# Infini-attention beside an FNet block: new times for the projections' helper work, a new table of a group's operations, another block order at the end

## The chip, the cores and the metric

The kernel runs on one core of a Trainium2 chip. The metric is the device time of one execution in microseconds (us). A core has a matrix engine (TensorE; PE in the profile, PEld for its weight loads), a vector engine (DVE), a scalar engine (ACT), a general engine (POOL) and a queue engine that issues the transfers (SP). Each engine takes its instructions strictly in the order in which they stand in its own queue, and an instruction that waits holds up all that stand behind it.

## What is computed

Two independent blocks over 2048 rows of 576 features, whose results are laid side by side. Cut to what matters:

```python
# A: 32 heads of 18, 4 segments s of 512 rows
q, k, v = x @ wq, x @ wk, x @ wv
for s in range(4):
    logits = q_s @ k_s.T * scale + mask   # mask: -1e9 where the key comes after the query
    a_dot  = softmax(logits) @ v_s
    a_mem  = (phi(q_s) @ M) / (phi(q_s) @ z + 1e-6)
    o_s    = g * a_mem + (1 - g) * a_dot
    M, z   = M + phi(k_s).T @ v_s, z + sum(phi(k_s))
out_A = concat(o_s) @ wo
# B
a, b  = xB @ hid_re.T, xB @ hid_im.T
out_B = seq_re @ a - seq_im @ b
```

The result has to be close to float32. So most operands are cut into a high and a low half, high by a copy to a narrower type on ACT, low by a subtraction on DVE or POOL, and a product is two or three matrix multiplications.

## The kernel before

Three stages follow each other.

**Projections (0 to about 237 us of the span).** For each of the four segments: nine products of queries and keys (`project_qk`, L368 and L148, the copy out of PSUM at L426) and four blocks of values (`project_v`, L483 to L495), with the memory's sums (`accumulate`, L522), the lookup in it (`lookup`, L555 to L576) and a transposed copy of the keys for it (`k_natural`, L464, which reads the key tiles `kf` that L426 writes). Each segment has 13 ticks: nine for the products, four for the value blocks. Beside this main line there is helper work with a written time each, in ticks from the start: load, high and low half of the other block's input (`fourier_load`, `fourier_high` L295 on ACT, `fourier_low` L300 on DVE), high and low half of the keys (L396 ACT, L402 DVE) and of the queries (L393 and L394 ACT, L400 POOL), load and split of the next segment's input (`x_load`, `split_x`: L121 ACT, L122 DVE). The table `TIMES` holds these times. They are sorted into one agenda, and after each tick `timed` issues all that is due, so the table alone decides behind which main instructions a piece of helper work stands on its engine.

**Attention and the Fourier block together (about 237 to 895 us).** Attention works on 32 groups of four heads, the Fourier products are a stream of matrix multiplications (`dense`: first `hidden`, L858 to L868, then `sequence`, L814, evacuated at L879). A group step has 16 slots. `PLACE` gives each operation of a group a place in slots, and 16 more mean one step later. In each slot the operations due are issued, and then as much of `dense` as keeps the two streams even. So the table also decides how many dense multiplications lie between two attention multiplications on PE. `PLAN` holds a few extra pieces by slot: among them the load and split of the second set of hidden weights (`h_load`, `h_split`, L594).

The path of one group, named as in the table:
- `run_1` to `run_4` are what PE does: scores (L1202) into the PSUM banks `s` and `t`, two of each. `run_1` writes f1 and s0, `run_2` f0 and s1, `run_3` s2, f2 and the transposed scores t1 (L1287), `run_4` t0 and t2. A run waits until the readers of its banks are done. `run_2` and `run_4` also hold the sums with the values (L1334, L1335), `run_4` ends with a small transposition of the maxima.
- `f_min`, `s_min` (L1210, DVE) take row minima from PSUM; `f_exp` (L1232, L1236, ACT) follows `f_min` and leaves `pf`.
- `f_hi` (L1244, ACT) and `f_lo` (L1249) cut `pf` into the tile `hl`. `f_turn` (L1253) transposes a half of `hl` by a transfer from SP's queue into `ptt`. There is one `hl` for each half, so the next group's `f_hi_1` waits for that transfer.
- `maxima` (POOL) and `maxima_out` (L1270, ACT) hand the row maxima to the transposed side, whose bank `t` they read.
- `t_exp` (L1294, L1298, ACT), `t_mask` (L1302, POOL), `t_hi` (L1307, ACT) and `t_lo` (L1314) make `phi` and `plo` for the sums with the values.
- `pv_read` (L1341, L1342, DVE) and `pv_out` (POOL, L1351 to L1357) finish a head.
- `stacks`, `values`, `memory` are loads. `c_cut` (L645 ACT, and its low half on POOL, which runs from the line of the delayed calls, L192) prepares the next operand `cs` of the dense stream, about five times in a step.

`LOW` says which of DVE and POOL makes each low half. Before, `f10`, `f11`, `f21`, `t20` and `t21` were POOL's, the rest DVE's.

**Output (about 911 to 971 us).** The product with `wo` by seventh-part sums (L1100). Then the branch: a flag `passed` is loaded, and if it is 0 the Fourier block is computed again in a general way (`fourier_by_words`). With the inputs here the flag is 1 and the block is skipped.

Of the kernel before, what the change touches and what calls it, by code (L numbers as in the profile page):

```python
# [101 lines left out]
def infini_attention_and_fnet(ctx: ExitStack, tc: tile.TileContext, xT, wqk, w8, wv, wo, beta, xbT, cT, hT, out):  # L102
# [582 lines left out]
    def value_load(G):  # L685
        if G < NG:
# [3 lines left out]

    TIMES = {
        "fourier_load": [
            2.22, 2.55, 6.61, 6.23, 11.7, 12.08, 14.63, 15.65, 19.32, 18.99, 22.59, 22.5, 24.9, 26.14, 28.77, 29.86,
            34.38, 33.5, 36.97, 36.61],
        "fourier_high": [
            3.55, 5.07, 8.15, 7.45, 13.2, 13.58, 16.57, 16.92, 21.57, 20.49, 24.09, 24.66, 27.16, 27.59, 30.27, 31.36,
            35.09, 35.6, 38.47, 38.32],
        "fourier_low": [
            4.72, 5.52, 9.13, 8.76, 13.83, 14.45, 18.15, 17.99, 21.9, 21.58, 24.28, 25.96, 27.52, 27.84, 31.66, 32.51,
            36.55, 36.26, 39.65, 38.97],  # L700
        "key_high": [
            6.72, 12.35, 9.68, 12.09, 5.49, 22.11, 19.18, 22.09, 26.12, 21.34, 33.23, 34.06, 38.2, 37.41, 33.04, 45.1,
            45.51, 50.28, 48.1, 44.1],
        "key_low": [
            7.72, 12.69, 10.68, 13.09, 6.98, 22.12, 25.68, 23.09, 26.75, 21.83, 34.6, 38.89, 41.52, 37.46, 34.47,
            46.1, 46.51, 51.28, 51.89, 45.1],
        "query_high": [
            6.49, 7.59, 12.09, 11.79, 19.0, 23.0, 23.22, 25.91, 33.32, 39.28, 33.75, 37.62, 45.14, 46.73, 50.47, 48.38],
        "query_low": [
            8.39, 7.92, 12.86, 11.89, 19.1, 23.33, 23.95, 26.32, 33.42, 39.38, 33.85, 38.03, 45.24, 46.83, 50.57,  # L710
            48.48],
        "x_load": [
            8.47, 8.76, 9.32, 10.61, 11.01, 15.83, 16.51, 19.4, 22.78, 24.1, 26.63, 31.84, 32.51, 33.4, 33.84],
        "x_split": [
            9.78, 10.88, 24.46, 24.08, 30.02, 32.47]}
    AGENDA = []

    def begin_cut(what, n):
# [715 lines left out]
    for i in BOTH:  # L1434
# [7 lines left out]
    WORK["stacks"], WORK["values"], WORK["memory"] = stack_load, value_load, memory_load  # L1442

    PLACE = {
# [8 lines left out]
    LOW = {k: (dve, pool)[n] for k, n in {  # L1453
        "f00": 0, "f01": 0, "f10": 1, "f11": 1, "f20": 0, "f21": 1, "t00": 0, "t01": 0, "t10": 0, "t11": 0, "t20": 1,
        "t21": 1}.items()}

    def attention():
# [45 lines left out]
    output_stage(prepare)  # L1503
    stages.close()
    rv = nc.values_load(passed, min_val=0, max_val=1)
    with tc.If(rv < 1, preferred_fallthrough_block=False):
        fourier_by_words(tc, dma, xbT, cT, hT, out)


# [41 lines left out]
```

## Time and profile before

| | |
|---|---|
| time, median of 3 runs | 972.62 us (972.52 to 977.6) |
| the profiled execution | 972.7 us, of which the span from first to last instruction is 970.9 us |
| PE busy | 925.2 us, 95% of the span |
| DVE, ACT, POOL busy | 738.6, 695.9, 652.5 us |
| mean granted clock of TensorE | 0.987 |

How to read it: a row of a group names the line, the engine, the operation and the tiles, then how often, the busy time in us and the mean length in ns, then the idle time just before and who ended it. A row of the waits says who waited for whom, the sum in us, how often, and the longest. A row of a timeline has the start in us, the length, the instruction, and in brackets how long the engine stood idle before it and who released it. PEclk is the granted clock of TensorE as a share of its full one. PE's own busy time counts overlapping ends of its multiplications, so a PE that is busy all the time still has the pace of its multiplications as its limit.

### The profile page before, as it was taken

To read this page: it belongs to the slowest core of one execution; us is meant where nothing else is said; L and a number is where in the kernel's file an instruction comes from. 1 tells how busy PE (TensorE), PEld (TensorE's weight loads), DVE (VectorE), ACT (ScalarE), POOL (GpSimd) and SP (SyncE) were. 2 spreads that over 40 slices of the span, in tenths; PEclk is the share of its full clock that TensorE was granted. 3 is DMA by queue.
4 is the path that set the end of the run, shared out by engine and by line. 5 is a ranking of instruction groups with operands and counts; after the bars stand their busy time and mean duration, and the time that the engine had idled before them with its cause. 6 is when DMAs were issued, how large, how long until landed. Compare 5 with 4: busy or idle time off the path is not lost.

```text
span 970.9 us, 25747 instructions
## 1 busy us (share of the span) xinstructions
PE 925.2 (95%) x9288; PEld 737.4 (76%) x9288; DVE 738.6 (76%) x1994; ACT 695.9 (72%) x1665; POOL 652.5 (67%) x954
## 2 busy tenths in 40 slices
PE   9999898998899999999899999999999999999996
PEld 8988888987677777777677777777776767777896
DVE  7777876877787777787677877777777788886783
ACT  6777757675576777887678788788778877886341
POOL 1566655676233335886778888878878998878560
PEclk9999998999999999999999999999999999999999
DMA  8565655656857655777797987888889797776552
GB/s 259 174 195 157 223 167 166 220 166 239 232 111 162 136 127 145 166 182 183 181 210 177 208 215 186 180 206 211 183 210 225 191 205 181 192 183 144 165 171 86
DMA packets 283129, 177.69 MB, mean 183 GB/s; under 512 B 204881, under 2 KB 240977, under 8 KB 282961
## 3 DMA queue, kind: packets, MB, share of 16 engines
q1 hardware_dynamic: 282768, 175.82, 70.9%
q8 instruction: 75, 1.23, 0.5%
q14 instruction: 62, 0.50, 0.2%
q10 hardware_dynamic: 224, 0.14, 0.1%
HBM read 90.00 MB, written 44.83 MB: 139 GB/s over the span
## 4 chain that ended last, share of the span: by engine, by line
PE 47%; ACT 17%; POOL 13%; DVE 8%; DMA 8%; issue 6%; SPq 0%; POOLq 0%; DVEq 0%; ACTq 0%
PE d L814 17%; DMA ptt<-hl 4%; PE d L858 3%; PE qk L368 3%; ACT pd L1298 3%; PE d L859 3%; PE d L860 3%; POOL cs L192 3%; PE t L1100 2%; PE pv L1334 2%; PE v L148 2%; ACT hl L1244 2%; ACT phi L1294 2%; ACT cs L645 2%; DVE s L1210 2%
## 5 line engine op out<-in xcount | busy, mean ns | idle before, releaser
L814 PEld LDWEIGHTS <-cs 128*128 128x128 f16 x3072 | 293.6, 98 | 89.4 <-issue 18.0
L814 PE MATMUL d<-wide,cs 128*128 128x288 f16 x2592 | 338.8, 287 | 4.5 <-ACT y L879 4.5
L1210 DVE CUSTOM_DVE_ANT_0 s<-s,causal 128x384 f32<-128x384 f32 (+2 forms) x320 | 147.2, 501 | 87.0 <-PE s L1202 57.4
L1249 POOL TENSOR_TENSOR hl<-pf,hl 128x512 f16<-128x512 f32 (+1 forms) x96 | 101.1, 1061 | 116.0 <-ACT hl L1244 106.1
L192 POOL TENSOR_TENSOR cs<-craw,cs 128x512 f16<-128x512 f32 x128 | 157.5, 1236 | 31.5 <-ACT cs L645 25.5
L1236 ACT ACTIVATE pf<-s,nb 128x384 f32<-128x384 f32 (+3 forms) x256 | 117.4, 525 | 3.2
L1244 ACT ACTIVATE hl<-pf 128x512 f16<-128x512 f32 (+1 forms) x192 | 94.0, 555 | 14.1 <-DMA ptt<-hl 13.9
L1249 DVE TENSOR_TENSOR hl<-pf,hl 128x512 f16<-128x512 f32 (+1 forms) x96 | 80.6, 874 | 30.5 <-ACT hl L1244 29.4
L1210 DVE CUSTOM_DVE_ANT_0 t<-t,causal 128x384 f32<-128x384 f32 (+1 forms) x192 | 98.9, 543 | 2.2
L645 ACT ACTIVATE cs<-craw 128x512 f16<-128x512 f32 x128 | 80.6, 634 | 2.3 <-PE d L814 2.3
L1294 ACT ACTIVATE phi<-t 128x384 f16<-128x384 f32 x128 | 63.7, 498 | 13.0 <-PE t L1287 9.5
L1232 ACT ACTIVATE nb<-nb 128x2 f32<-128x2 f32 (+1 forms) x96 | 19.5, 203 | 66.4 <-DVE nb L1210 66.3
L814 PE MATMUL d<-ab,cs 128*128 128x288 f16 x480 | 66.2, 286 | 0.0
L1314 POOL TENSOR_TENSOR plo<-pd,phi 128x384 f16<-128x384 f32 x64 | 58.3, 926 | 2.4 <-ACT pd L1298 2.4
L1202 PEld LDWEIGHTS <-st 54*128 54x128 f16 x512 | 20.3, 94 | 49.3 <-issue 43.3
L148 PE MATMUL v<-wide,xh 128*128 128x288 f32 x256 | 54.7, 306 | 0.4 <-ACT r L426 0.4
L1314 DVE TENSOR_TENSOR plo<-pd,phi 128x512 f16<-128x512 f32 x64 | 53.7, 870 | 1.5 <-ACT phi L1307 1.4
L868 ACT ACTIVATE wide<-d 128x288 f16<-128x288 f32 x54 | 22.3, 415 | 35.5 <-PE d L865 35.4
L1302 POOL TENSOR_SCALAR_AFFINE_SELECT pd<-pd 128x512 f32<-128x512 f32 x64 | 44.7, 721 | 0.3 <-ACT pd L1298 0.2
L368 PE MATMUL qk<-xh,wide 128*128 128x512 f32 x128 | 44.1, 401 | 0.0
L1314 DVE TENSOR_TENSOR plo<-t,phi 128x384 f16<-128x384 f32 x64 | 33.6, 553 | 12.9 <-ACT t L1298 12.6
L148 PEld LDWEIGHTS v<-wide,xh 128*128 128x128 f32 x256 | 41.9, 193 | 1.0 <-ACT r L426 0.6
(329 smaller groups left out, 2466.2 us busy)
## 6 DMA issues: line engine op xcount, KB each, us to landing
craw<-cT SPq DMA_DIRECT2D x128, 256.0 KB
vd<-vs SPq DMA_DIRECT2D x16, 440.0 KB
vst<-vd SPq DMA_DIRECT2D x32, 220.0 KB
st<-qd SPq DMA_DIRECT2D x64, 108.0 KB
st<-kd SPq DMA_DIRECT2D x64, 108.0 KB
wide<-xbT SPq DMA_DIRECT2D x20, 256.0 KB
xk<-xd SPq DMA_DIRECT2D x20, 256.0 KB
out<-y SPq DMA_DIRECT2D x16, 288.0 KB
```

What stands on the lines that cost most here:

```text
L148: pe.matmul(o, a, b, start=n == 0, stop=n == len(terms) - 1)
L192: fn(*a)
L368: pe.matmul(FIRST[m], *terms[m][n], start=n == 0, stop=n == 13)
L645: act.activation(t[:, 0], raw, AF.Copy)
L814: pe.matmul(o[h], a, b[:, h * 288:h * 288 + 288], start=start, stop=stop)
L1210: dve.tensor_tensor_reduce(x, x, CAUSAL[0][:, L - w:], scale=scale, scalar=-LOWEST, op0=OP.add, op1=OP.min, accum_out=into[:, 4 * half + i ...
L1236: act.activation(f[kind][half][:, to:to + w], o[half][:, c:c + w], AF.Exp, bias=nb[:, 4 * half + i:4 * half + i + 1], scale=-1.0)
L1244: act.activation(hl[half][:, 0, F_COL[kind]:F_COL[kind + 1]], f[kind][half], AF.Copy)
L1249: engine.tensor_tensor(hl[half][:, 1, a:b], f[kind][half], hl[half][:, 0, a:b], OP.subtract)
L1294: act.activation(t[0][:, a:a + 384], x, AF.Exp, bias=LIFT, scale=SCALE)
L1302: pool.affine_select(v, v, pattern=[[0, 4], [1, P]], base=0, channel_multiplier=-1, compare_op=OP.is_ge, fill=0.0)
L1314: engine.tensor_tensor(lo[:, a:b], f, hi[:, a:b], OP.subtract)
```

## The change

Three things change, and no instruction of the computation is added or left out.

1. All the times in `TIMES` are new, most by less than a tick, some by two to five ticks.
2. `PLACE` is new, and in `LOW` the low halves f10, f11 and f21 go from POOL to DVE, t00 and t01 from DVE to POOL.
3. The block of the branch that is never taken here is placed directly behind the main block, where before the empty block was.

```diff
     TIMES = {
...
         "x_split": [
-            9.78, 10.88, 24.46, 24.08, 30.02, 32.47]}
+            9.48, 11.3, 19.05, 24.61, 32.55, 34.01]}
...
     PLACE = {
-        "stacks": -10.31, "run_1": 1.0, "f_min_1": 1.1, "s_min_0": 2.05, "f_exp_1": 3.7, "run_2": 6.0, "f_min_0": 6.1,
...
+        "stacks": -8.87, "run_1": 1.4, "f_min_1": 1.74, "f_exp_1": 2.61, "s_min_0": 4.8, "run_2": 5.08, "f_min_0":
...
     LOW = {k: (dve, pool)[n] for k, n in {
-        "f00": 0, "f01": 0, "f10": 1, "f11": 1, "f20": 0, "f21": 1, "t00": 0, "t01": 0, "t10": 0, "t11": 0, "t20": 1,
+        "f00": 0, "f01": 0, "f10": 0, "f11": 0, "f20": 0, "f21": 0, "t00": 1, "t01": 1, "t10": 0, "t11": 0, "t20": 1,
         "t21": 1}.items()}
...
-    with tc.If(rv < 1, preferred_fallthrough_block=False):
+    with tc.If(rv < 1, preferred_fallthrough_block=True):
         fourier_by_words(tc, dma, xbT, cT, hT, out)
```

In the new file every line behind the first table has a number higher by one, so L1249 of before is L1250 now.

What it does to the order shows best at three places. The rows are instructions of one engine in the order of its queue, with the line, the operation, and out<-in by tile names.

**The third segment's last products, on ACT.** `kf` is the copy of a product out of PSUM, the last of the four being the one that `k_natural` needs first. Before:

```order
L295 ACTIVATE p<-wide 128x512
L426 ACTIVATE kf<-qk 128x512
L121 ACTIVATE xh_136<-raw 128x512
L426 ACTIVATE kf<-qk 128x512
L396 ACTIVATE p<-kf,sc 128x512 x2
L393 ACTIVATE q<-q,sc 128x512
L394 ACTIVATE p<-q 128x512
L393 ACTIVATE q<-q,sc 128x512
L394 ACTIVATE p<-q 128x512
L426 ACTIVATE kf<-qk 128x512
```

The same place now:

```order
L295 ACTIVATE p<-wide 128x512 x2
L426 ACTIVATE kf<-qk 128x512 x2
L396 ACTIVATE p<-kf,sc 128x512
L121 ACTIVATE xh_135<-raw 128x512
L393 ACTIVATE q<-q,sc 128x512
L394 ACTIVATE p<-q 128x512
L426 ACTIVATE kf<-qk 128x512
L396 ACTIVATE p<-kf,sc 128x512
L426 ACTIVATE kf<-qk 128x512
L121 ACTIVATE xh_136<-raw 128x512
```

Between the last but one `kf` and the last there stood two key halves and two query cuts; now one key half stands there, one query cut comes before both, and an input split comes after them.

**The first step of attention, on ACT.** `ab<-raw` at L594 is `h_split`, which waits for a weight load; the `pf` of 128x512 are `f_exp_0`. Before:

```order
L868 ACTIVATE wide<-d 128x288
L594 ACTIVATE ab<-raw 128x576
L868 ACTIVATE wide<-d 128x288
L1232 ACTIVATE nb<-nb 128x2
L1236 ACTIVATE pf_3294<-s,nb 128x512
L1236 ACTIVATE pf_3295<-s,nb 128x512
```

Now:

```order
L869 ACTIVATE wide<-d 128x288 x2
L1233 ACTIVATE nb<-nb 128x2
L1237 ACTIVATE pf_3278<-s,nb 128x512
L1237 ACTIVATE pf_3279<-s,nb 128x512
L594 ACTIVATE ab<-raw 128x576
```

`f_exp_0` has passed the split that waits for a transfer.

**A late group, on DVE, from the last minimum after `run_3` to the end of the step.** `hl` is written by `f_lo`, `plo` by `t_lo`, `pw` and `pa` by `pv_read`. Before:

```order
L1314 TENSOR_TENSOR plo<-t,phi 128x384 x2
L1341 RECIPROCAL pw<-pv 128x8
L1342 TENSOR_REDUCE pa<-pv 128x144
L1249 TENSOR_TENSOR hl<-pf_9498,hl 128x512
L1249 TENSOR_TENSOR hl<-pf_9578,hl 128x256
L1249 TENSOR_TENSOR hl<-pf_9499,hl 128x512
```

Now:

```order
L1250 TENSOR_TENSOR hl<-pf_9374,hl 128x512
L1250 TENSOR_TENSOR hl<-pf_9375,hl 128x512
L1315 TENSOR_TENSOR plo<-t,phi 128x384 x2
L1250 TENSOR_TENSOR hl<-pf_9575,hl 128x256
L1250 TENSOR_TENSOR hl<-pf_9475,hl 128x512
L1250 TENSOR_TENSOR hl<-pf_9476,hl 128x512
L1250 TENSOR_TENSOR hl<-pf_9576,hl 128x256
```

The two low halves f10 and f11 now stand ahead of `t_lo_10` and `t_lo_11`, which free the banks `t` for `run_4`, and f21 has come behind; `pv_read_0` has moved ahead of `run_3`'s minima, and the two `t_lo` of kind 0, which stood on DVE between `run_1` and `run_2`, are POOL's. On PE, the dense multiplications between the runs, on the mean of the groups 8 to 30, go from 35, 28, 27 and 21 (behind `run_1`, `run_2`, `run_3`, `run_4`) to 27, 20, 35 and 28; their sum in each step is the same.

More of the change, by code (lines that the diff above doesn't have):

```diff
@@ L698, in infini_attention_and_fnet @@
+            35.23, 34.44, 38.71, 40.14],
         "fourier_low": [
-            4.72, 5.52, 9.13, 8.76, 13.83, 14.45, 18.15, 17.99, 21.9, 21.58, 24.28, 25.96, 27.52, 27.84, 31.66, 32.51,
-            36.55, 36.26, 39.65, 38.97],
+            4.94, 4.99, 9.42, 7.61, 11.58, 12.85, 18.13, 17.97, 21.45, 21.42, 24.28, 25.96, 27.25, 28.51, 31.81,
+            31.55, 36.51, 34.59, 39.28, 40.59],
         "key_high": [
-            6.72, 12.35, 9.68, 12.09, 5.49, 22.11, 19.18, 22.09, 26.12, 21.34, 33.23, 34.06, 38.2, 37.41, 33.04, 45.1,
@@ L703, in infini_attention_and_fnet @@
-            45.51, 50.28, 48.1, 44.1],
+            7.19, 12.35, 9.7, 13.5, 5.18, 22.47, 19.18, 22.79, 26.59, 21.05, 33.59, 35.2, 38.62, 37.17, 32.23, 45.1,
+            46.49, 50.73, 48.1, 44.1],
         "key_low": [
-            7.72, 12.69, 10.68, 13.09, 6.98, 22.12, 25.68, 23.09, 26.75, 21.83, 34.6, 38.89, 41.52, 37.46, 34.47,
-            46.1, 46.51, 51.28, 51.89, 45.1],
+            7.56, 12.69, 10.84, 15.71, 6.17, 22.51, 26.54, 23.97, 26.87, 21.54, 34.69, 38.89, 41.96, 37.58, 32.39,
+            46.1, 47.97, 51.28, 51.89, 45.1],
@@ L707, in infini_attention_and_fnet @@
         "query_high": [
-            6.49, 7.59, 12.09, 11.79, 19.0, 23.0, 23.22, 25.91, 33.32, 39.28, 33.75, 37.62, 45.14, 46.73, 50.47, 48.38],
+            6.49, 8.34, 12.49, 10.17, 19.12, 25.56, 25.1, 26.13, 32.73, 38.45, 36.68, 37.33, 46.92, 47.19, 49.45,
+            48.01],
         "query_low": [
-            8.39, 7.92, 12.86, 11.89, 19.1, 23.33, 23.95, 26.32, 33.42, 39.38, 33.85, 38.03, 45.24, 46.83, 50.57,
+            6.99, 8.67, 13.26, 10.27, 19.22, 25.89, 25.83, 26.98, 32.95, 38.55, 36.78, 37.74, 50.46, 47.29, 49.55,
@@ L711, in infini_attention_and_fnet @@
             48.48],
         "x_load": [
[L713 removed]
+            8.44, 8.76, 9.32, 10.17, 10.77, 16.17, 16.51, 19.52, 24.06, 24.1, 26.04, 29.19, 31.69, 35.39, 36.94],
         "x_split": [
[L715 removed]
+            9.48, 11.3, 19.05, 24.61, 32.55, 34.01]}
     AGENDA = []
```

7 lines of the change are left out of this document (3 added, 4 removed), and 14 rows, old and new, of the table PLACE.

## The prediction

> **What bounds the kernel now.** I read the page's busy times first, then the stretches by stage, then the waits of PE. The times are those of the profiled execution, 972.7 us around a span of 970.9; the median of the runs, 972.62, is the same to 0.1 us, so a difference worked out here holds for both.
>
> ```profile
> PE 925.2 (95%) x9288; PEld 737.4 (76%) x9288; DVE 738.6 (76%) x1994; ACT 695.9 (72%) x1665; POOL 652.5 (67%) x954
> ```
>
> ```profile
> 0.00:237.00 237.00, 225.64 (x1373) 202.68 (x1374) 181.44 (x360) 166.90 (x365) 140.10 (x218) 0.98 0.61 196
> 237.00:262.00 25.00, 21.43 (x148) 14.74 (x147) 18.88 (x55) 12.71 (x31) 8.34 (x12) 0.86 0.76 236
> 262.00:394.00 132.00, 129.00 (x1456) 97.03 (x1455) 104.84 (x324) 95.54 (x240) 54.51 (x92) 1.00 0.61 137
> 394.00:623.00 229.00, 221.74 (x2660) 164.55 (x2658) 173.47 (x546) 181.07 (x443) 185.01 (x266) 0.99 0.83 193
> 623.00:874.00 251.00, 240.47 (x2884) 178.81 (x2882) 198.85 (x597) 200.27 (x488) 214.94 (x304) 1.00 0.85 197
> ```
>
> PE is the bound in every stage, and the change leaves its multiplications as they are. So all that can be won is PE's idle time: 237 - 225.6 = 11.4 us in the projections, 3.6 in the first step, 3.0 in the seven steps with `hidden`, and 7.3 + 10.5 = 17.8 in the later ones, 36 us in all. Beside it there is time at a lower clock:
>
> ```profile
> 116.00:120.00 4.00, 4.00 (x18) 3.71 (x19) 3.79 (x14) 1.44 (x4) 1.73 (x2) 0.57 0.90 216
> 154.00:161.00 7.00, 6.36 (x28) 6.37 (x29) 3.93 (x8) 4.04 (x11) 4.34 (x7) 0.51 0.90 289
> 253.00:257.00 4.00, 3.69 (x20) 2.21 (x19) 3.43 (x12) 2.48 (x6) 2.84 (x3) 0.57 0.51 137
> 485.00:489.00 4.00, 4.00 (x28) 2.45 (x27) 2.71 (x6) 3.97 (x11) 3.50 (x9) 0.57 1.02 270
> ```
>
> The clock is 0.57 on the mean of 4 us, which is half speed for 3.4 of them: 1.7 us of work lost each time, and 0.49 x 7 = 3.4 us in the long one. Each of these stretches begins beside one of PE's longest waits, as at 485:
>
> ```profile
> 484.02 2.19 PE L814 MATMUL d<-wide,cs 128*128 128x288 f16 x13 [3.82 <-ACT y L879]
> ```
>
> The waits by sum, times and the longest:
>
> ```profile
> PE t L1202 <- ACT mt L1270: 10.6, 18, 1.5
> ACT ab L594 <- DMA raw<-hT: 5.2, 1, 5.2
> PE d L814 <- ACT y L879: 4.5, 3, 3.8
> PE kt L464 <- ACT kf L426: 3.8, 2, 3.2
> PE s L1202 <- ACT pf L1236: 3.1, 4, 2.0
> PE look L561 <- DVE vr L486: 3.0, 3, 2.2
> ```
>
> The waits of 2.2 us (`look`), 3.2 (`kt`), 2.0 (`s`) and 3.8 (`d`) are the four that have a slow stretch behind them; the 18 short ones on `mt` have none. I go through the change by these rows.
>
> **The projections' times.** The `look` wait comes from a heap on DVE at the end of a value block of the second segment:
>
> ```profile
> 111.15 0.68 DVE L122 TENSOR_TENSOR xl<-raw,xh 128x512 fp32r<-128x512 f32 x1
> 111.75 1.66 DVE L300 SCALAR_TENSOR_TENSOR p<-wide,p 128x512 f16<-128x512 f32 x1
> 113.33 1.74 DVE L122 TENSOR_TENSOR xl<-raw,xh 128x512 fp32r<-128x512 f32 x1
> ```
>
> `x_split`'s third time goes from 24.46 to 19.05, so one of the two `xl` leaves this heap for a tick in which DVE had no helper work. That is 0.7 to 1.7 us; the one that goes stands last, so I take 1.7, and half of the slow stretch (0.9), since 0.5 us of wait stays: -2.6.
>
> The `kt` wait is the heap on ACT that the order shows:
>
> ```profile
> 147.93 0.62 ACT L121 ACTIVATE xh<-raw 128x512 fp32r<-128x512 f32 x1
> 150.45 0.72 ACT L396 ACTIVATE p<-kf,sc 128x512 f16<-128x512 f32 x1 [0.81 <-POOL sc L386]
> 154.01 0.58 ACT L426 ACTIVATE kf<-qk 128x512 f32<-128x512 f32 x1
> ```
>
> From the first row to the last are eight operations in 6.1 us, 0.8 of them a wait, so some 0.6 us each. Ahead of the last `kf` one query cut (two operations), a key half and an input split go elsewhere: 2.4 us of the 3.2. With half of the slow stretch, 1.7, that is -4.1. What moved earlier lands in ticks 30 to 32 and DVE's tick 34, which now holds three low halves instead of two; one of about 1 us late at the next `look` would be a wait of its own, and the loads that come up to two ticks earlier meet the weights' loads. I put +2 on both together, between 0 and the 4 us of the waits now removed. The first step:
>
> ```profile
> 250.89 0.68 ACT L594 ACTIVATE ab<-raw 128x576 f16<-128x576 f32 x1 [5.21 <-DMA raw<-hT]
> 252.00 1.26 ACT L1236 ACTIVATE pf<-s,nb 128x512 f32<-128x512 f32 x2
> ```
>
> `f_exp_0` stands behind a split that sat 5.2 us for its load, and `run_3` waits for `f_exp_0` (2.0 and 0.3 us). Now it stands before the split. The split still waits, but behind it are only evacuations `wide<-d`, for which PE has three banks: -2.3, and half of a slow stretch, -0.9.
>
> **The group's table.** On PE the distance from `run_4` to the next `run_1` grows from 21 to 28 dense multiplications. Their pace:
>
> ```profile
> 605.94 3.85 PE L814 MATMUL d<-wide,cs 128*128 128x288 f16 x30
> 609.62 0.90 PE L814 MATMUL d<-ab,cs 128*128 128x288 f16 x6
> ```
>
> 30 in 3.68 us, so 0.123 us each and 0.86 us more for seven. The 18 waits on `mt` (`maxima_out`, which frees bank `t` for s0) are 0.6 us on the mean: nearly all go, -10.6 at most; I take that. These also hold in the `hidden` steps.
>
> The wait of 3.8 us at 480 us begins with a transfer:
>
> ```profile
> ACT hl L1244 <- DMA ptt<-hl: 13.9, 10, 3.5
> ```
>
> `f_hi_1` sat 3.5 us for the other half's transposition, ACT with it, and behind it the cut of the next `cs`. All low halves that `f_turn_0` needs are now done about two slots earlier (2.4 us: 394 to 874 us are 25 steps, 19.2 us for 16 slots) on the queue, `f_hi_1` is asked for one slot earlier. So this wait goes but with one slot of room: -3.8 and half a slow stretch, -0.9.
>
> What is late next is DVE. Between `run_3` and `run_4` it now has two more low halves ahead of `t_lo_10` and `t_lo_11`:
>
> ```profile
> 615.80 0.39 PE L1202 MATMUL s<-st 54*128 54x256 f16 x4
> ```
>
> ```profile
> 617.83 1.02 DVE L1314 TENSOR_TENSOR plo<-t,phi 128x384 f16<-128x384 f32 x2
> ```
>
> ```profile
> L1249 POOL TENSOR_TENSOR hl<-pf,hl 128x512 f16<-128x512 f32 x64 | 73.2, 1156 | 100.4 <-ACT hl L1244 91.9 <-DMA out<-y 3.8 <-DMA craw<-cT 3.8
> L1249 DVE TENSOR_TENSOR hl<-pf,hl 128x512 f16<-128x512 f32 x64 | 64.7, 1012 | 29.5 <-ACT hl L1244 29.4
> ```
>
> The minima are through 617.83 - 615.80 = 2.0 us after `run_3` begins, 2.2 with the next instruction's start; then 2 x 1.01 and 1.02 makes 5.2 us. PE comes to the multiplication that needs the bank after the runs' own 0.5 us, 35 x 0.123 = 4.3, and 0.25 for t0: 5.0. So it waits about 0.2 us in each of 25 steps, +5. Between `run_1` and `run_2` there are 27 multiplications instead of 35, 3.3 us behind 0.9 of `run_1` itself, 4.2:
>
> ```profile
> 623.73 0.39 PE L1202 MATMUL s<-st 54*128 54x384 f16 x4
> ```
>
> ```profile
> 626.45 1.57 ACT L1236 ACTIVATE pf<-s,nb 128x384 f32<-128x384 f32 x4
> ```
>
> `f_exp_1` ended 628.02 - 623.73 = 4.3 us after `run_1` began, so that is even: +0.1 a step, +2.5. `t_lo_00` and `t_lo_01` on POOL:
>
> ```profile
> L1314 POOL TENSOR_TENSOR plo<-pd,phi x64: 903/912/1356, 283.3 to 892.3; 128x384 f16<-128x384 f32 x64
> L1314 DVE TENSOR_TENSOR plo<-pd,phi x64: 650/691/1643, 287.8 to 895.0; 128x512 f16<-128x512 f32 x64
> L1314 DVE TENSOR_TENSOR plo<-t,phi x64: 546/553/559, 276.6 to 886.4; 128x384 f16<-128x384 f32 x64
> ```
>
> Four `t_lo` of 0.9 to 1.2 us and one or two `cs` now stand on POOL before `run_2`'s sums; in an average step they are done, now and then not: +2.5. In sum POOL gives 2 x 1.16 + 0.87 us a step and takes two of about 1.2, DVE gives 2 x 0.87 (mean) and takes 2 x 1.01 + 0.6: DVE goes from 199 of 251 us busy to about 83%, POOL from 86 to 82%. Bounds of these three new waits: 0 if the low halves on DVE run at 0.65 (the shortest row above), and 37 us if each needs 1.64 (the longest): 2.2 + 3.3 + 1.0 = 6.5, 1.5 us late, 25 times. I take +10, near the mean row.
>
> Here the Trainium skill speaks against the change. "SBUF — State Buffer", section "Who interferes with whom", says that a DVE instruction with both inputs in SBUF contends with a GpSimd instruction that reads SBUF, and that the loser is held for the other's whole length. The rows agree: 546 to 559 ns with one input in PSUM, 650 to 1643 with both in SBUF. By that rule with POOL 82% busy in 1.16 us pieces a low half would take some 0.65 + 0.5 = 1.15 us (an estimate), the wait at `run_4` 0.5 us, and the time 967.
>
> **The branch.** One far jump is on SP's path before and after:
>
> ```profile
> L1506 SPq COMPARE_BRANCH x2: 43/50/57, 965.0 to 966.3; - x2
> L1544 SPq EVENT_SEMAPHORE x10: 17/28/28, 969.5 to 970.8; - x10
> ```
>
> The jump takes 969.5 - 966.3 = 3.2 us and came after the wait for the last store (1.3 us from the first branch). Now the jump comes first and the store lands meanwhile: -0.5, between -1.3 and +3.2, the last if the short second jump costs as much.
>
> **The sum.** -2.6 - 4.1 + 2 - 3.2 - 10.6 - 4.7 + 10 - 0.5 = -13.7, from 972.7: 959.
>
> **The rivals.**
> - *DVE becomes the bound between `run_3` and `run_4`* (slower). With a wait of 1.0 us there in 25 steps, instead of 0.2, the sum is -13.7 + 20 = +6: 979. It decides from 0.75 us a step, that is from a low half of 1.3 us. For it speaks the 1.64 us row; against it that the mean with POOL at 85% is 1.01, and that DVE has over a microsecond idle behind `f_lo_21` to catch up. 11 in 100.
> - *The waits only change place* (no change). PE's waits on `mt` come back as waits on `f_min` and `f_exp`, whose distances became shorter, and half of the projections' gain too: -13.7 + 10.6 + 3 = 0: 970 to 973. For it: 0.0 us of room between `run_1` and `run_2`. 17 in 100.
> - *All slow stretches go and DVE keeps up*: the other halves of them, 0.9 + 1.7 + 0.9 + 0.9 = 4.4 us more, and +2 instead of +10: 947. 12 in 100.
> - *The slow stretches don't hang on these waits*: 963, still faster; held in my forecast.
>
> The skill's page "TensorE: Matmul & The Clock Gate", Part 1, says that the clock is halved after an idle window of about 3.4 us. By it the waits of 2.0 and 2.2 us would be too short, their stretches would stay, and the time would be 961; here stretches follow such waits, so I keep the rows.
>
> **How the numbers follow.** My forecast, 950 to 967, has 60 in 100. Less than 0.5% (4.9 us) is what a measurement of this kernel cannot tell from no change. Faster than that: 60 + 12 = 72; within it: 17; slower: 11. The range goes from 948, near the fastest case, to 973, where the case of no change ends; the likeliest alone has 950 to 967.
>
> **What would show it.** Right: no wait of `t` on `mt` over 1 us in total; the wait of `kt` at the third segment under 1 us; no stretch at 0.57 at 253 and at 485; new waits of PE on `plo` from DVE or on bank `t` at `run_4`, some 0.2 us each; low halves f10 and f11 near 1.0 us. Wrong: group steps longer than 19.2 us; DVE over 90% in the last stretch; a new wait over 2 us in the projections, with its own slow stretch.

## The result, and the profile after

The changed kernel takes 959.81 us on the median of four runs (956.91 to 960.03), the kernel before 973.01 beside it (972.52 to 977.6): a ratio of 0.985, with a 95% interval of 0.981 to 0.988. The forecast was 959. The profiled execution is the 956.91 one, with a span of 955.2, so differences between the two traces (15.7 us) are some 2.5 us more than those of the medians. The kernel after has one line more, so its L1203 is L1202 of before, and so on.

The first part of the page, the busy times:

```profile
PE 920.7 (96%) x9288; PEld 731.4 (77%) x9288; DVE 739.8 (77%) x2026; ACT 698.6 (73%) x1665; POOL 629.2 (66%) x922
```

PE is still the bound. The stages, now cut at the starts of the same instructions in both traces (run_1 of step 0, of step 1 and of step 7, the end of the last sums). Columns as in the prediction: the stretch, its length, busy times of PE, PEld, DVE, ACT, POOL, granted clock, DMA share, GB/s. First the kernel before, then the kernel after:

```profile
0.00:237.08 237.08, 225.65 (x1374) 202.68 (x1374) 181.52 (x360) 166.98 (x365) 140.18 (x218) 0.98 0.61 196
237.08:262.14 25.06, 21.56 (x148) 14.74 (x147) 18.94 (x54) 12.63 (x31) 8.40 (x12) 0.86 0.76 237
262.14:394.70 132.56, 129.56 (x1459) 97.42 (x1460) 104.80 (x324) 96.24 (x242) 55.07 (x94) 1.00 0.62 137
394.70:897.63 502.93, 484.38 (x5822) 361.26 (x5822) 386.48 (x1164) 395.93 (x964) 419.47 (x593) 1.00 0.83 193
897.63:970.90 73.27, 64.06 (x490) 61.31 (x488) 46.90 (x94) 24.10 (x65) 29.34 (x41) 0.97 0.44 140
```

```profile
0.00:231.95 231.95, 221.74 (x1373) 198.32 (x1374) 177.41 (x360) 167.18 (x365) 141.17 (x218) 1.00 0.63 200
231.95:255.86 23.91, 20.67 (x148) 14.17 (x148) 19.79 (x58) 13.20 (x32) 6.37 (x9) 0.93 0.76 242
255.86:385.73 129.87, 129.04 (x1459) 97.03 (x1458) 108.44 (x332) 96.50 (x243) 52.41 (x87) 1.00 0.64 141
385.73:881.69 495.96, 484.43 (x5816) 359.98 (x5816) 386.87 (x1184) 397.13 (x961) 398.72 (x567) 1.00 0.84 196
881.69:955.20 73.51, 64.81 (x496) 61.90 (x494) 47.26 (x95) 24.61 (x67) 30.48 (x44) 0.96 0.44 139
```

The stages give 5.1, 1.2, 2.7 and 7.0 us, and the end takes 0.2 back: 15.7 (the rounded terms make 15.8). In the projections PE's idle time fell only from 11.4 to 10.2; the other 3.9 us are busy time, and time at half clock is what went there (0.98 to 1.00). In the late steps it is the other way round: the busy time is equal, and the idle time went from 18.6 to 11.5. DVE is busy for 387 of 496 us there, 78%, no bound.

The waits of PE in the kernel after, whole span (sum, times, longest):

```profile
PE pv L1336 <- POOL plo L1315: 4.9, 6, 1.6
PE kt L464 <- ACT kf L426: 2.4, 4, 1.0
PE look L555 <- DVE vr L486: 2.4, 2, 1.4
PE s L1288 <- ACT pf L1237: 2.2, 7, 1.0
PE s L1203 <- ACT pf L1237: 2.2, 7, 0.4
PE qk L368 <- DVE vr L486: 1.7, 1, 1.7
PE t L1203 <- DVE negm L1211: 1.4, 2, 1.1
PE t L1203 <- ACT mt L1271: 1.4, 2, 1.1
```

`mt` went from 10.6 us in 18 waits to 1.4 in 2, and the wait of `d` on `y` (4.5 in 3) is no longer in the list. The sums `pv` wait more for `plo`: 4.9 us, all on POOL's, where the kernel before has 1.2 in 2 on DVE's and 0.8 in 1 on POOL's. The wait of `qk` at the start of the second segment is new. The list leaves out what PE's busy time covers, the overlapping ends of its multiplications; in the steps that matters, as the distances between starts show further down.

The half-speed stretches went further than forecast in this execution. Before had five (one of them double), by the granted clock 10.2 us of work lost in all; after has one ahead of its end, from 242.8 to 246.2, 1.7 us lost. What calls one up shows in pairs of windows of 3.4 us, each time the window ahead of a stretch and the one behind it. Of the kernel before:

```profile
113.10:116.50 3.40, 1.21 (x10) 1.01 (x9) 3.40 (x6) 2.12 (x6) 1.42 (x1) 1.00 0.57 210
116.50:119.90 3.40, 3.40 (x16) 3.11 (x15) 3.19 (x12) 1.44 (x4) 1.63 (x2) 0.51 0.88 197
...
481.80:485.20 3.40, 1.18 (x10) 0.95 (x10) 0.00 (x0) 2.77 (x9) 1.54 (x2) 1.00 0.70 224
485.20:488.60 3.40, 3.40 (x16) 2.00 (x14) 2.34 (x5) 3.37 (x9) 2.90 (x9) 0.50 1.01 256
```

and of the kernel after, in its one stretch and at its new wait on `qk`:

```profile
239.39:242.80 3.41, 1.84 (x12) 0.98 (x12) 2.97 (x10) 0.71 (x3) 0.00 (x0) 1.00 0.99 333
242.80:246.20 3.40, 3.40 (x16) 2.06 (x15) 2.70 (x12) 2.00 (x4) 0.00 (x0) 0.50 0.89 260
58.50:61.90 3.40, 1.71 (x8) 1.14 (x7) 1.91 (x5) 3.29 (x9) 0.00 (x0) 1.00 0.87 327
61.90:65.30 3.40, 3.40 (x18) 2.84 (x17) 3.37 (x6) 3.31 (x6) 2.60 (x2) 1.00 0.01 4
```

With PE busy for 1.2 of 3.4 us the next window ran at half clock; with 1.71 and 1.84, about half, it went once one way and once the other. How many stretches there are changes from one execution to the next, too. Ahead of step 0 the six traces with the old times (before, e2, e3, e4, e7, e10) have 2 or 3 windows at half clock, 2.7 on the mean, and the six with the new ones (after, e1, e8, e11, e12, e13) 0 to 2, 0.8 on the mean; the profiled execution of the kernel after is one of the two with none.

### The profile page after: what moved, and what is told of

It is laid out like the page before. It is cut to its first block, busy times and chain, and to the rows that moved or that the text cites. A ratio compares the mean times of both kernels' runs of the same rounds, so it can differ in the third digit from the quotient of the medians.

```text
span 955.2 us, 25678 instructions
## 1 busy us (share of the span) xinstructions
PE 920.7 (96%) x9288; PEld 731.4 (77%) x9288; DVE 739.8 (77%) x2026; ACT 698.6 (73%) x1665; POOL 629.2 (66%) x922
## 4 chain that ended last, share of the span: by engine, by line
PE 47%; ACT 12%; POOL 6%; DVE 5%; issue 4%; DMA 2%; ACTq 0%; POOLq 0%; DVEq 0%
PE d L815 21%; PE pv L1335 4%; PE d L859 3%; PE d L861 3%; PE d L860 3%; ACT pf L1237 3%; PE t L1101 2%; PE s L1203 2%; DMA ptt<-hl 2%; DVE s L1211 2%; POOL plo L1315 2%; PE pv L1336 2%; ACT hl L1245 2%; ACT pd L1299 2%; PE s L1101 2%
## 5 line engine op out<-in xcount | busy, mean ns | idle before, releaser
L1211 DVE CUSTOM_DVE_ANT_0 s<-s,causal 128x384 f32<-128x384 f32 (+2 forms) x320 | 147.9, 500 | 84.9 <-PE s L1203 35.0
L192 POOL TENSOR_TENSOR cs<-craw,cs 128x512 f16<-128x512 f32 x128 | 150.9, 1179 | 71.3 <-ACT cs L645 69.0
L1250 DVE TENSOR_TENSOR hl<-pf,hl 128x512 f16<-128x512 f32 (+1 forms) x192 | 142.5, 789 | 14.4 <-ACT hl L1245 14.2
L1315 POOL TENSOR_TENSOR plo<-pd,phi 128x384 f16<-128x384 f32 (+1 forms) x128 | 130.4, 1039 | 7.9 <-ACT phi L1308 6.6
L1259 POOL CAST mb<-negm 128x8 bf16<-128x8 f32 x32 | 18.0, 562 | 73.7 <-DVE negm L1211 73.7
L1303 POOL TENSOR_SCALAR_AFFINE_SELECT pd<-pd 128x512 f32<-128x512 f32 x64 | 45.2, 728 | 22.2 <-ACT pd L1299 22.2
L1203 PEld LDWEIGHTS <-st 54*128 54x128 f16 x512 | 19.7, 94 | 42.1 <-issue 35.9
L1203 PE MATMUL s<-st 54*128 54x256 f16 (+3 forms) x320 | 43.9, 296 | 3.9 <-ACT pf L1237 2.2
L368 PE MATMUL qk<-xh,wide 128*128 128x512 f32 x128 | 43.5, 396 | 1.7 <-DVE vr L486 1.7
L1336 PE MATMUL pv<-vst,plo 128*128 128x37 bf16 x640 | 37.8, 179 | 4.9 <-POOL plo L1315 4.9
L148 PE MATMUL qk<-xh,wide 128*128 128x512 f32 x128 | 42.0, 389 | 0.0
L1308 ACT ACTIVATE phi<-pd 128x512 f16<-128x512 f32 x64 | 37.9, 619 | 4.7 <-POOL pd L1303 4.7
```

The costliest lines, as they stand in the source:

```text
L148: pe.matmul(o, a, b, start=n == 0, stop=n == len(terms) - 1)
L192: fn(*a)
L1203: pe.matmul(o[half][:, first + c:first + c + w], q[r, x, i * P:w], k[r, x, :w], start=True, stop=True)
L1211: dve.tensor_tensor_reduce(x, x, CAUSAL[0][:, L - w:], scale=scale, scalar=-LOWEST, op0=OP.add, op1=OP.min, accum_out=into[:, 4 * half + i ...
L1250: engine.tensor_tensor(hl[half][:, 1, a:b], f[kind][half], hl[half][:, 0, a:b], OP.subtract)
L1315: engine.tensor_tensor(lo[:, a:b], f, hi[:, a:b], OP.subtract)
```

## The experiments

In the table each kernel's profiled execution is cut at the same instructions, in us: to the first key transposition of the second segment's value blocks ("to key 2"), from there to that of the third ("to key 3"), on to run_1 of step 0, step 0, the steps with `hidden`, the later ones to the last sums, the rest. The times are ratios to the kernel before on the same chip, with their intervals.

| kernel | to key 2 | to key 3 | to step 0 | step 0 | hidden | late | end | ratio |
|---|---|---|---|---|---|---|---|---|
| before | 88.4 | 62.5 | 86.2 | 25.1 | 132.6 | 502.9 | 73.3 | |
| after | 91.4 | 58.5 | 82.1 | 23.9 | 129.9 | 496.0 | 73.5 | 0.985 (0.981 to 0.988) |
| e1_times | 91.2 | 58.6 | 83.3 | 25.2 | 132.6 | 503.9 | 73.3 | 0.996 (0.994 to 0.998) |
| e2_table | 89.9 | 63.3 | 84.9 | 22.4 | 129.6 | 496.1 | 73.8 | 0.990 (0.987 to 0.993) |
| e3_branch | 89.5 | 61.5 | 86.2 | 26.9 | 132.6 | 502.5 | 72.5 | 0.999 (0.997 to 1.002) |
| e4_place_old_low | 89.7 | 63.3 | 86.3 | 23.1 | 131.1 | 526.0 | 74.5 | 1.024 (1.019 to 1.029) |
| e10_low_only | 88.6 | 62.4 | 86.2 | 24.7 | 133.2 | 554.9 | 74.8 | 1.053 (1.050 to 1.057) |
| e5_one_split | 89.6 | 60.8 | 84.9 | 24.1 | 132.6 | 502.6 | 73.6 | 0.998 (0.996 to 1.001) |
| e6_third | 89.5 | 63.4 | 87.5 | 22.5 | 132.6 | 502.5 | 72.9 | 1.002 (1.000 to 1.005) |
| e7_hsplit | 89.5 | 63.0 | 86.4 | 21.0 | 132.6 | 502.0 | 74.1 | 0.998 (0.995 to 1.000) |
| e8_mt_late | 92.9 | 58.6 | 84.3 | 23.6 | 133.7 | 498.0 | 75.4 | 0.993 (0.990 to 0.996) |
| e11_run2 | 91.3 | 59.2 | 83.5 | 23.2 | 129.6 | 496.3 | 73.0 | 0.987 (0.984 to 0.990) |
| e12_run2_block5 | 90.2 | 60.2 | 82.4 | 23.9 | 129.9 | 500.2 | 73.4 | 0.986 (0.983 to 0.989) |
| e13_run2_slot | 92.0 | 59.3 | 82.1 | 23.3 | 130.5 | 494.6 | 72.7 | 0.984 (0.982 to 0.987) |

Rows that share the code of a stage show how far it varies by itself: with the old times the stretch to key 3 lies between 61.5 and 63.4 (e5 apart), and step 0 of the old places between 22.5 and 26.9 (e7 apart). The steps with `hidden` repeat to 0.3 us. So step 0 of one trace says little by itself; on the mean it takes 24.7 us with the old places (e7 apart) and 23.3 with the new ones.

**The three parts alone.** `e1_times`, `e2_table` and `e3_branch` are the kernel before with one of the new `TIMES`, the new `PLACE` and `LOW`, and the new `preferred_fallthrough_block`.

> Before with the new projection times alone. My theory: PE's two long waits in the projections and the two slow stretches behind them are what the times remove, so the first group begins about 5 us earlier than before (237.1 us there), nothing changes behind that, and the run is 5 us shorter: 967 to 969. Rival, the waits only change place: the first group begins earlier, but the attention steps, whose order is the old one, take it back, 971 to 973.

> Before with the new table of a group's operations and the new sharing of the low halves alone. My theory: -3 us in the first step (the split that waited for a load), -3 in the hidden steps and -4 to -6 in the later ones, together -10, so 961 to 965; the first group begins at 237 as before. Rival, the table won only together with the times: 968 to 971.

> Before with the other block order alone. My theory: SP's far jump overlaps the landing of the last store, and from the last vector operation to the end of the span it takes 7.4 us in place of 7.9: -0.5 us, 972.4. Rival, a second jump costs as much as the first: +2 to +3 us, 975.

0.9958 x 0.9898 x 0.9993 = 0.985: the product of the parts is the whole, so within the intervals, some 0.003 each, none is seen to depend on another. By these ratios the times give 4.1 us of 972.6, the table 9.9, both inside their theory's range (968.5 and 962.7). The gain of the times is not one of clock alone: the trace of e1 has six windows at half clock ahead of its end, as many as the kernel before. The branch gives 0.7 with an interval that reaches to 1.002; in its trace the last stage is 0.8 us shorter.

**The table's halves.** `e4_place_old_low` has the new places and the old sharing of the low halves, `e10_low_only` the reverse.

```
e4:   PLACE of after, LOW of before
e10:  PLACE of before, LOW of after
```

> Before with the new places but the old sharing: f10, f11, f21 on POOL, the four low halves of kind 0 of the other side on DVE. My theory: what counts are the distances of the runs on PE and what stands ahead of what, so most of the gain of the table stays, but POOL is again held by the low halves that wait for a transposition, 2 to 4 us slower than with the new sharing: 965 to 968. Rival, DVE was made the bound by the new sharing: then this is faster than the new table by 3 us or more, 958 to 961.

> The kernel before with the new sharing of the low halves between DVE and POOL, and the old places. The new places with the old sharing took 1.024. Theory (places and sharing hang together: a low half on DVE must not stand ahead of the minima that PE's next runs wait for): at the old places f_lo_10 (9.38) and f_lo_11 (10.28) now stand on DVE about `f_min_2` (10.2) and hold it up to wait for ACT, so PE gets new waits of 0.3 to 0.8 us a step at run_4 or at the next run_1, while the waits on `mt` stay: 5 to 15 us slower (1.005 to 1.015). Rival (the sharing alone carries the gain, by taking the t_lo off DVE ahead of the new minima): 3 to 8 us faster (0.992 to 0.997).

Both are slower than before, 1.024 and 1.053, where both together are faster, 0.990. The first was missed by its theory and its rival alike, and the second lost 52 us instead of 5 to 15. The waits of e4:

```profile
ACT nb L1232 <- DVE nb L1210: 104.6, 63, 3.1
DVE plo L1314 <- ACT phi L1307: 68.5, 28, 5.1
PE s L1202 <- ACT pf L1236: 21.6, 37, 1.8
```

and of e10:

```profile
POOL mb L1258 <- DVE negm L1210: 168.0, 31, 18.2
DVE s L1210 <- PE s L1202: 101.5, 58, 8.1
PEld L1335 <- POOL plo L1314: 49.9, 42, 3.0
PE pv L1335 <- POOL plo L1314: 45.0, 41, 2.9
```

In e4 DVE itself sits at `t_lo_00` and `t_lo_01` for ACT's `phi`, 68.5 us in 28 waits, and behind them in its queue are run_1's minima; so ACT's `f_exp_1` is late (it is `nb` that `f_exp_1` begins with), and PE waits for it 37 times (21.6 us against 3.1 before). In e10 these two are POOL's, but at the old places `t_lo_01` stands just ahead of `run_2` (37.81, that is 5.81 of a later step, against 6.0), whose sums need it: 41 waits, 45 us. So the new sharing needs the new places and the reverse. Neither is a part that brings half of the gain.

**The wait on `look`.** One number of the kernel before.

```
-  x_split: 9.78, 10.88, 24.46, 24.08, 30.02, 32.47
+  x_split: 9.78, 10.88, 19.05, 24.08, 30.02, 32.47
```

> The kernel before with one number changed: the third time of x_split goes from 24.46 to 19.05. Theory (a heap on DVE makes the wait of 2.2 us on `look` at the end of the second segment): the wait falls to about 0.5 us, the half-speed stretch at 116 to 120 us goes or is halved, the third segment's first transposition starts 1.7 to 3.4 us earlier than 150.9, and the time is 2.6 us less than before (0.997). Rival (the `xl` only blocks DVE in its new place, near the start of the segment): a new wait of 1 to 2 us between 88 and 105 us, and no change of the time within 1 us.

The window of the wait and the next one, and PE's wait there:

```profile
113.10:116.50 3.40, 3.37 (x28) 3.14 (x26) 3.33 (x7) 3.29 (x8) 2.35 (x3) 1.00 0.54 194
116.50:119.90 3.40, 2.91 (x20) 2.73 (x21) 3.24 (x11) 2.54 (x8) 2.16 (x2) 1.00 0.79 249
```

```profile
PE look L561 <- DVE vr L486: 0.8, 2, 0.5
```

The wait fell from 2.2 to 0.5 us as forecast, and the half-speed stretch at 116 us is gone. That the edit took the stretch away is not shown by this: e3 and e10 have the old times, the wait of 2.2 us and no stretch there either, and e5 has another one at 93 us, as e10 has. In e3 the same wait falls across two of the windows of 3.41 us in which the clock changes (the last section has them):

```profile
113.07:116.48 3.41, 2.35 (x19) 2.12 (x17) 3.41 (x3) 3.38 (x9) 3.06 (x2) 1.00 0.39 145
116.48:119.90 3.42, 2.30 (x17) 2.25 (x18) 3.33 (x11) 1.87 (x6) 1.05 (x1) 1.00 0.83 212
```

The kernel before has PE busy for 1.21 us in the window of this wait, and half clock behind it; e3 has 2.35 and 2.30, and full clock. The part to key 3 is 2.2 us shorter than in e7, measured with it, which has the same times there otherwise, and 0.7 us shorter than the shortest of the other kernels with the old times; of the whole time the interval, 0.996 to 1.001, tells no more than that 2.6 us is possible.

**The wait on `kt`.** The kernel before with these times:

```
key_high[11] 34.06 -> 35.2     key_high[14], key_low[14]     33.04, 34.47 -> 32.23, 32.39
x_split[4:]  30.02, 32.47 -> 32.55, 34.01
query_high[8], query_low[8]    33.32, 33.42 -> 32.73, 32.95
query_high[10], query_low[10]  33.75, 33.85 -> 36.68, 36.78
```

> The kernel before with nine times changed, all of loads and cuts about the third segment's start: two key blocks (12 and 15), two query cuts (9 and 11) and the last two input splits. Theory (the wait of 3.2 us on `kt` is a heap on ACT): the third segment's start stays at 150.9, the wait falls below 1 us, the half-speed stretch at 154 to 161 us is halved or goes, and the first group step starts 3 to 4 us earlier than 237.1; time 0.996 of before. Rival (the projections' gain comes from the other times, or the moved work makes a new heap two ticks earlier): the step starts within 1 us of 237.1.

The rival held: no gain. PE's waits about the third segment's value blocks, and ACT ahead of the longer one:

```profile
PE look L561 <- DVE vr L486: 3.3, 1, 3.3
PE kt L464 <- ACT kf L426: 0.8, 1, 0.8
```

```profile
163.22 0.63 ACT L295 ACTIVATE p<-wide 128x512 f16<-128x512 f32 x1 [3.25 <-DMA wide<-xbT]
```

`kt` fell from 3.2 to 0.8 us and its stretch went, as the theory has it. But ACT then stood 3.25 us at the high part of block 16 of xbT, whose transfer had not landed, and the wait came back at the next `look`, 3.3 us with a double stretch behind it. In the kernel before the same operation starts at 162.64 without a wait: the stall ahead of it had hidden the late transfer. In the kernel after, blocks 16 and 17 are loaded 0.9 and 1.5 ticks earlier, and ACT waits 0.5 us at them. So the key and query cuts and the input splits alone, which is all that this edit moves, don't carry the gain. That they need the loads that move with them is argued from this wait; no run adds those loads alone.

**The first step.** The kernel before, with the first split of hT's second part behind `f_exp_0`.

```
-            at(0, 6 + 3 * k, h_split, 1, k)
+            at(0, 6 + 3 * k + 2 * (k == 0), h_split, 1, k)
```

> The kernel before with the first split of hT's second part two slots later, so that `f_exp_0` of the first step stands ahead of it on ACT. Theory: PE's wait of 2.0 us at run_3 (s on pf) goes, the half-speed stretch at 253 to 257 us with it, and the first step is 2.3 to 3.2 us shorter than 25.1; time 0.997 of before. Rival (ACT has then to make up the 5.2 us of the split's wait elsewhere; only the wait's place changes): the step is 0 to 1.2 us shorter, the time within 1 us of before.

Step 0 takes 21.0 us instead of 25.1, shorter than in any other kernel, and PE's wait on `pf` is gone from it, with the stretch at 253 us; the ratio, 0.9975, makes 2.4 us, between 0.4 and 4.6 by its interval. So the wait is removed, as the theory has it, and the step is 3.8 us below the mean of the old places, 24.7. How much of this is the stretch stays open: in e5, where PE's wait on `pf` is 2.8 us, it falls across two windows and has no stretch behind it. The step of the kernel after takes 23.9. The waits of the kernel after in that step:

```profile
PE t L1203 <- DVE negm L1211: 1.4, 2, 1.1
PE t L1203 <- DVE w L574: 1.3, 1, 1.3
PE s L1203 <- DVE vr L486: 0.9, 1, 0.9
PE s L1203 <- ACT pf L1237: 0.5, 2, 0.4
```

`s_min_0` now stands just ahead of `run_2`, which needs its bank `t`: 1.4 us, and with the 0.5 on `pf` enough idle time in one window for a half-speed stretch.

**The waits on `mt`.** The kernel after with `maxima_out` at 16.96 again.

> The kernel after with one number put back: `maxima_out` at 16.96 instead of 15.52, so it stands 0.44 slots ahead of the next `run_1` on ACT instead of 1.9. Theory (PE's waits on `mt`, 10.6 us in the kernel before, come from how late ACT comes to `maxima_out` ahead of `run_1`): waits of 0.3 to 0.6 us come back in most of 25 steps, 5 to 11 us more than the kernel after, a ratio of 0.990 to 0.996. Rival (what took them away is the 28 dense multiplications between run_4 and run_1 instead of 21): no waits on `mt`, the ratio of the kernel after, 0.985, within 0.002.

The waits on `mt` of this kernel, in the steps with `hidden` and in the late ones:

```profile
PE t L1203 <- ACT mt L1271: 3.0, 6, 0.9
...
PE t L1203 <- ACT mt L1271: 1.9, 3, 1.1
```

The kernel before has 3.0 us in 6 and 7.6 in 12 there, the kernel after none and 1.4 in 2. So in the steps with `hidden` it is the place of `maxima_out` that takes the waits away, as the theory has it (3.8 us longer with the old place), and in the late steps most are gone with the old place too, which leaves the 28 dense multiplications, as the rival has it. The time is inside the theory's range, 0.993, 6.5 us above the 960.9 of e11 measured beside it; some 2 of these are a longer end stage, which the edit doesn't touch, and whose cause stays open.

**A later run_2.** Three kernels ask whether the new waits at `run_2` can be placed away.

```
e11:  run_2 5.08 -> 5.6, f_min_0 5.74 -> 5.9
e12:  as e11, and fourier_load[5], high[5], low[5]  10.21, 11.71, 12.85 -> 12.08, 13.58, 14.45
e13:  run_2 5.08 -> 6.0, f_min_0 5.74 -> 6.1
```

> The kernel after with `run_2` at 5.6 instead of 5.08 and `f_min_0` at 5.9 instead of 5.74: some 0.6 us more between run_1 and run_2. In the trace of the kernel after, `f_exp_1` ends 4.29 us after run_1 begins, run_2 begins 4.08 us after it on the median, and run_2 to run_3 has 4.85 us for a chain that takes 3.37. Theory (the change's largest new waits, 8.5 us on `f_exp_1` and 6.0 on POOL's `plo`, stand at run_2 and are only a matter of its place): they fall to 2 to 4 us in sum, the time is 7 to 12 us below the kernel after, a ratio of 0.973 to 0.978. Rival (the waits change place to run_3, whose chain now begins later): within 3 us of the kernel after, 0.982 to 0.988.

The 8.5 and 6.0 us in it are reckoned from the distances between starts of PE's instructions and count delays below the size that the list of waits has. The expectation was idle: the places act by whole slots and by their order, 5.08 and 5.6 are both slot 5, and the program came out the same on every engine. So this is a second time of the kernel after: 960.9 us, 0.987 against 0.985, and a span of 956.0. It tells how well two ratios agree here (0.0025, 2.5 us), and its half-speed stretches lie elsewhere: 154 and 236 us instead of 242.8.

> As the one with the later run_2, and the three times of the sixth block of xbT's load (load, high part, low part) put back from 10.21, 11.71 and 12.85 to 12.08, 13.58 and 14.45. In the kernel after, ACT waits 1.27 us at 58.6 us for that block's transfer, and PE 1.7 us at 59 us behind it, at the second segment's start. Theory: that wait goes and nothing comes in its place: 1.5 to 3 us less than with the later run_2 alone. Rival (the block's work then meets the second segment's first ticks): no difference within 1 us.

The wait on `qk` fell from e11's 2.3 us to 0.8, and the stretch to key 2 is 1.1 us shorter, but a half-speed stretch at 93 us gave that back by key 3. Step 0 begins 1.2 us earlier than in e11. Two more such stretches in the late steps, at 752 and 773 us, where the program is that of e11, took this too. No difference in the time: 0.986 against 0.987.

> The kernel after with `run_2` at 6.0 and `f_min_0` at 6.1, so that run_2 is moved behind the dense multiplications of slot 5; the places act by whole slots and by their order, and the earlier try with 5.6 and 5.9 moved nothing on any engine, so its 960.9 is a second time of the kernel after. On PE run_2 now stands some 9 multiplications (1.1 us) later. Theory (the largest new waits of the kernel after, 8.5 us on `f_exp_1` and 6.0 on POOL's `plo` ahead of run_2's sums, are only a matter of run_2's place): run_1 to run_2 goes from 4.08 to about 5.1 us on the median, above f_exp_1's 4.29, run_2 to run_3 from 4.85 to about 4.0, above the chain's 3.37; the two waits fall to 4 us or less in sum, the time is 6 to 12 us lower, a ratio to before of 0.974 to 0.981. Rival (the waits change place to run_3, whose room falls to 0.6 us): 0.983 to 0.989.

Here run_2 does move: run_1 to run_2 goes from 4.08 to 5.06 us on the median, as expected. But run_2 to run_3 falls to 3.14, not to 4.0, below the 3.37 that the chain to `f_exp_0` needs. The waits of its steps:

```profile
PE pv L1336 <- POOL plo L1315: 3.9, 4, 2.0
PE s L1288 <- ACT pf L1237: 1.9, 4, 1.0
PE t L1203 <- ACT mt L1271: 1.6, 3, 1.1
```

The sums' wait on `plo` fell by 1 us only, and the small waits on `f_exp_1` turned into others: by the distances between starts, in the table of the next section, `run_2`'s scores take 7.5 us less than in the kernel after, and those of `run_3` and `run_4` 5.3 more. At 956.81 us and a ratio of 0.984 it is the fastest of all kernels tried, 0.003 below e11, but the intervals overlap: no gain over the kernel after is shown, and the ratio lies in the rival's range.

## Why the prediction was right

The time was within 1 us of the forecast, but some terms were off in size, and part of those errors cancel. By its steps:

- *Projections, -2.6 - 4.1 + 2 = -4.7*: measured -5.1. To key 3 (without the start) 4.1 came instead of 2.6, behind it 4.1 as forecast. The price of new clusters was +3.0 instead of +2, up to key 2. What differs is where the gain lies: in this trace the stretches went whole, 5.1 us of lost work instead of the 2.6 of "half of the slow stretch", while the idle time fell by 1.2 only. On the means of the kernels with the old and the new times 1.8 windows fewer are at half clock, 3.1 us, so the half was near.
- *First step, -3.2*: measured -1.2 in this trace, and -1.4 on the means of the kernels with the old and the new places. The wait on `f_exp_0` fell from 2.3 us to 0.5. The prediction did not have the wait of `run_2` on `s_min_0`, 1.4 us: it looked at the bank `s` there and not at `t`. Behind this wait stands the one stretch that is left, 1.7 us; e2 has the wait without a stretch, and its step takes 22.4. Nor did the prediction count the stretch that the kernel before has at 239.4 us, behind the waits of 1.0 and 1.2 us with which this step begins: it names four stretches, and there are five.
- *The steps behind it, -10.6 - 4.7 + 10 = -5.3*: measured -9.7. The list of waits is too small a base for these terms, as PE's busy time covers part of the delays. The distances between the starts of neighbouring multiplications hold all of it. Summed over the steps 1 to 30 (the other 1.4 of the 9.7 us lie behind them), in us, by the run that the distance leads to or comes from:

| kernel | run_1 | scores of run_2 | sums of run_2 | scores of run_3 and run_4 | sums of run_4 | between dense ones | in all |
|---|---|---|---|---|---|---|---|
| before | 38.2 | 20.7 | 35.1 | 42.9 | 36.7 | 419.4 | 593.0 |
| after | 24.5 | 27.5 | 38.1 | 45.0 | 36.7 | 412.8 | 584.7 |
| e8_mt_late | 29.1 | 27.5 | 37.8 | 45.2 | 36.7 | 414.2 | 590.5 |
| e13_run2_slot | 24.7 | 20.0 | 37.5 | 50.3 | 36.7 | 414.9 | 584.2 |

The terms one by one, in this table:

- *The 18 waits on `mt`, -10.6*: -13.7 at `run_1`, where the list of waits has 9.2 less. The prediction gave it all to PE's distance; e8 shows that in the steps with `hidden` the earlier `maxima_out` does it.
- *The wait at 480 us, -4.7*: -6.6 between dense multiplications. The wait is gone, and its stretch whole.
- *The new waits, +10*: +6.8 at `run_2`'s scores, +3.0 at its sums and +2.1 at `run_3` and `run_4`, 11.9 in all. The sum was near, the parts were not, and this is the step of the prediction that was mis-sized. The wait at `run_2` on `f_exp_1`, forecast as +2.5, is the largest. A step of the kernel after, and `run_2` of the same step of the kernel before:

```profile
404.54 0.39 PE L1203 MATMUL s<-st 54*128 54x384 f16 x4
...
408.62 0.63 PE L1203 MATMUL s<-st 54*128 54x512 f16 x2
```

```profile
407.26 1.57 ACT L1237 ACTIVATE pf<-s,nb 128x384 f32<-128x384 f32 x4
```

```profile
417.67 0.39 PE L1202 MATMUL s<-st 54*128 54x512 f16 x2
```

`f_exp_1` ends 4.29 us after `run_1` begins, as reckoned (4.3), but `run_2` begins 4.08 after it on the median, not 4.2, and in 10 of the 23 groups from 8 to 30 at 3.83 or earlier. So its second multiplication waits, and the two take 0.63 us instead of 0.39. The wait of the sums on POOL's `plo` was forecast about right, +2.5. The one at `run_4`, forecast as +5, is nearly absent: on `plo` its bank waits 0.3 us by the list. What was too large there is the low half of 1.01 us. The row of DVE in the late steps of the kernel after:

```profile
L1250 DVE TENSOR_TENSOR hl<-pf,hl 128x512 f16<-128x512 f32 x100 | 78.6, 825 | 1.8 <-ACT hl L1245 1.8
```

The low half takes 0.825 us on the mean, and f10 and f11 take 0.85 and 0.72, 1.57 together instead of 2.02. These 0.45 us cover the 0.2 that was short.

The rule of the Trainium skill, "SBUF — State Buffer", section "Who interferes with whom", put a low half at 1.15 us and the time at 967, an estimate. The trace agrees that the two engines hinder each other, and not with the size of the estimate: reckoned over the kernel after, low halves of 128x512 that met no POOL instruction take 0.69 us on the mean of 14, those wholly beside POOL's work 1.18 on the mean of 20, and the longest of all takes 1.90; but the mean of those in the late steps is the 0.825 above.

- *The branch, -0.5*: the stretch from the last vector operation to the end is 0.5 us shorter in the trace after, and e3 gives 0.7 us of the time, not told from nothing. One jump of 3.5 us is on SP's path as before, and no second one came:

```profile
L1507 SPq EVENT_SEMAPHORE  x8: 17/17/17, 953.3 to 953.8; - x8
...
L1507 SPq COMPARE_BRANCH  x1: 57/57/57, 949.8 to 949.8; - x1
```

Of the signs that the prediction named, no stretch at 253 or at 485 us came out, and none of the signs of being wrong. The waits on `mt` are 1.4 us in all, not under 1, those of `kt` at the third segment 1.3 in two, the new waits stand at `run_2` and not at `run_4`, and f10 and f11 are shorter than 1.0.

By stage, what was measured less what was forecast is -0.4 in the projections, +2.0 in step 0, -4.4 in the other steps and +0.7 at the end: -2.1, in a trace that is some 2.5 us more favourable than the medians. So the hit is partly luck: too little gain was forecast in the later steps and too much in the first one, and among the new waits too much at `run_4` stands against too little at `run_2`.

Of the rivals, DVE as the bound between `run_3` and `run_4` is refuted: its wait there was to be 1.0 us a step, and the two runs take 2.1 us more in 30 steps; DVE is busy for 78%. That the waits only change place is true of e13, and of the change in part: the steps won 20.3 us at `run_1` and between dense multiplications, and 11.9 came back. "All slow stretches go" was nearest to what the clock did in this execution, 8.5 us of lost work instead of the 4.4 that the forecast counted; e11, the same program, has one window more. PE's busy time fell by only 4.5; part of the rest are delays that it covers, such as those at `run_2` (6.8 us by the starts, 0.9 more in the list), and the traces don't show what else. That the stretches don't hang on these waits is half true: the same wait has one or has none, by how it falls on the grid. The rule of the Trainium skill's "TensorE: Matmul & The Clock Gate", Part 1, an idle window of 3.4 us, would have no stretch behind waits of 2.0 and 2.2 us; the kernel before has them there, and e3 and e5 have such waits without one.

## What to carry to other kernels

Where one table sets both the order and the engine of some work, price the two together: here each half alone costs 2.4 and 5.3%, and the pair wins 1.0%. A helper moved for one queue needs its transfer moved too, and an earlier cut behind a load that has not landed only moves the wait (e6). Before trying a finer place, look whether the program's order changes at all.

## What was not expected of the hardware

The half-speed stretches hang on how busy PE is in a window of 3.41 us, on a grid: in the trace before, their starts are whole multiples of 3.413 us apart. The Trainium skill's "TensorE: Matmul & The Clock Gate", Part 1, has a free-running window of 3413 ns, and the trace agrees. Reckoned over the fourteen traces, without the slow start and the last stretch of each, from PE's records in each such window at full clock: with PE busy for less than 45% of it, the next window was at half clock in 36 of 36 cases; from 45 to 58% in 16 of 39; above that in 4 of 3779. So no idle window is needed here, only one that is less than about half busy, and a wait of about 2 us costs 1.7 us more or nothing, by where it falls on the grid: the wait of 2.2 us on `look` has a stretch behind it in the kernel before, where one window holds it (PE busy for 1.21 us), and none in e3, where two share it (2.35 and 2.30). This is read off, not tried: no experiment put a wait of a chosen length at a chosen place. It would also explain why the same program had its stretch at 242.8 us in one execution and at 154 and 236 in the other.
